# A recurrence and an MLP on one core: two bf16 transposes replaced by one fp32 transpose of channel pairs, with gates made before the turn and a set issue order

## The chip, the cores and the metric

The kernel runs on one core of one Trainium2 chip. The metric is device time in microseconds (us) of the whole program; lower is better. "Span" is the time from the first to the last instruction in a profiled execution, some 2 us less than the timed figure. Before the change the kernel took 444.84 us (median of 2 runs, 444.7 to 444.98).

PE is the matrix engine, PEld its weight loads (they overlap with matmuls), DVE the vector engine, ACT the scalar engine, POOL the general engine, SP the engine that only issues DMA here. SBUF is the on-chip working memory of 128 partitions, PSUM the memory that PE writes.

## The reference

```python
# x, f_logit: (4, 6144, 256) fp32; lower_bound: (256,); w1, w2: (256, 1024); w_out: (1024, 256)
sig = 1.0 / (1.0 + np.exp(-f_logit))
f = lower_bound + (1.0 - lower_bound) * sig
for t in range(S):                       # a recurrence along the tokens, per channel
    h = f[:, t] * h + (1.0 - f[:, t]) * x[:, t]
    y[:, t] = h
out = np.maximum(y @ w1, y @ w2) @ w_out # (24576, 256) fp32
```

Both kernels use u = sigmoid(-f_logit), so that 1 - f = (1 - lower_bound) u, and max(h1, h2) = h1 + relu(h2 - h1). So PE multiplies y by wd (the scaled difference of w2 and w1), ACT takes the relu, and PE multiplies that by w_out and adds y times w13 = w1 w_out.

## The kernel before

Tokens come in 48 blocks of 512. The inputs arrive with tokens on partitions; the recurrence is a scan along the free dimension, so channels have to be on partitions. PE turns both inputs, 128x128 at a time, in bf16 (the load casts from fp32 on the way).

```python
def load(c):                                   # cast to bf16 in the DMA, issued by POOL
    nat = inpool.tile([P, CH // P, D], BF16, name=name)
    nc.gpsimd.dma_start(out=nat[...], in_=src[b, t0:t0 + nt, :].rearrange("(i p) d -> p i d", p=P))
...
def turn(j, slot):                             # two bf16 transposes in each slot
    s, q = divmod(slot, FC // 2)
    if q == 0:
        turned[j, s] = ps_t.tile([P, KC, TB], BF16, name=("fT", "xT")[s])
    for h in range(KC):                        # KC = 2 channel halves
        nc.tensor.transpose(turned[j, s][:, h, q * P:(q + 1) * P],
                            ins[c][s][:, o * NSB + q, h * P:(h + 1) * P], ident_b[:])

def recurrence(j):                             # gates with channels on partitions
    nc.scalar.activation(out=u[:], in_=fT[:], func=AF.Sigmoid, scale=-1.0)
    nc.vector.tensor_tensor(out=v[:], in0=u[:], in1=xT[:], op=ALU.mult)
    for h in range(KC):
        nc.vector.tensor_scalar(out=ff[:, h, :], in0=u[:, h, :], scalar1=nom[:, h:h+1], scalar2=1.0, ...)
        nc.vector.tensor_tensor_scan(out=y[:, h, :], data0=ff[:, h, :], data1=v[:, h, :], ...)
...
# hidden(j, fc): two 128x512 matmuls into dT, relu by ACT into rt
# project(j, slot): five 128x256 matmuls into psO; weights are 128 tokens of y or rt
with tc.manual_schedule(engines={ENG.PE}):     # only PE's order is set, the rest is scheduled
    for j in range(NBLK + 1):
        for fc in range(FC):                   # FC = 8 slots of a block
            if j < NBLK: hidden(j, fc)
            if j > 0: project(j - 1, fc)
            if j + 2 < NBLK: turn(j + 2, fc)
        if j + 2 < NBLK: recurrence(j + 2)
```

## Time and profile before

| before | value | view |
|---|---|---|
| span | 443.3 us | page |
| PE busy | 95% | page, part 1 |
| chain of waits on PE | 94% | page, part 4 |
| a slot with two bf16 transposes | 1.09 us | timeline |
| a slot without any (last two blocks) | 0.975 us | timeline |
| first slot with all its parts (block 1, slot 1) | at 28.08 us | timeline |

The page of the kernel before. Its first line gives busy time, share of the span and number of instructions of each engine; the chain of waits is followed back from the last instruction, as shares of the span by engine and then by line.

```profile
PE 423.0 (95%) x3488; PEld 309.8 (70%) x3488; DVE 247.0 (56%) x345; ACT 278.5 (63%) x442; POOL 44.9 (10%) x57
...
PE 94%; DMA 4%; POOL 1%; DVE 0%; issue 0%; POOLq 0%
PE psO L227 47%; PE dT L202 37%; PE xT L103 5%; PE fT L103 5%; DMA wob<-in_moe_w_out_dram 4%; POOL fn L86 1%; POOL xn L86 1%; PE psO L186 0%; DVE osb L237 0%; POOL ident_f masks.py:199 0%; POOL ident_f masks.py:197 0%; POOLq masks.py:199 0%; POOLq L284 0%
```

PE is the bound. "Busy" alone does not prove it, since the records of matmuls overlap and their ends are modelled. The timeline does. This is PE in a steady stretch of the kernel before (start in us, length in us, engine, line, operation, names, shapes, count):

```profile
300.26 0.27 PE L103 MATMUL fT<-ident_b,fn 128*128 128x128 bf16 x2
300.38 0.59 PE L202 MATMUL dT<-y,wd 128*128 128x512 bf16 x2
300.81 0.71 PE L227 MATMUL psO<-wob,rt 128*128 128x256 bf16 x5
301.35 0.28 PE L103 MATMUL fT<-ident_b,fn 128*128 128x128 bf16 x2
301.46 0.38 PE L202 MATMUL dT<-y,wd 128*128 128x512 bf16 x1
```

Read the starts, not the lengths. A pair of 128x512 matmuls starts at 300.38 and the next at 301.46 (1.09 us when averaged over more slots): that is one slot. No idle time is noted in brackets behind any line. The last blocks have no transposes left to do:

```profile
425.94 0.59 PE L202 MATMUL dT<-y,wd 128*128 128x512 bf16 x2
426.37 0.71 PE L227 MATMUL psO<-wob,rt 128*128 128x256 bf16 x5
426.91 0.59 PE L202 MATMUL dT<-y,wd 128*128 128x512 bf16 x2
```

There a slot takes 426.91 - 425.94 = 0.97 us (0.975 to 0.98 over several slots). The difference of 0.11 us is what two bf16 128x128 transposes cost in the stream: 0.054 us each, although the record of one lasts 0.22 us.

The groups of instructions that the change touches (out<-in, shapes, count, then busy us and mean ns of one, then idle time of the engine before them and what ended it):

```profile
L127 DVE TENSOR_TENSOR_SCAN y<-ff,y,v 128x512 bf16<-128x512 bf16 x88 | 108.2, 1272 | 1.5
...
L103 PE MATMUL fT<-ident_b,fn 128*128 128x128 bf16 x384 | 52.2, 221 | 13.4 <-DVE ident_b L65 13.4
...
L103 PEld LDWEIGHTS <-fn 128*128 128x128 bf16 x384 | 37.3, 99 | 19.2 <-DMA fn<-in_f_logit_dram 11.0
...
L119 DVE TENSOR_SCALAR ff<-u,nom 128x512 bf16<-128x512 bf16 x96 | 29.9, 354 | 25.6 <-ACT u L113 25.6
...
L115 DVE TENSOR_TENSOR v<-u,xT 128x1024 bf16<-128x1024 bf16 x48 | 32.5, 677 | 3.9 <-PE xT L103 3.9
```

### The profile page before, as it was taken

How to read it: one execution, taken by the hardware profiler on the slowest of the kernel's cores; microseconds unless marked ns; L12 is line 12 of the kernel's file. 1: busy time of each engine (PE TensorE's matmuls, PEld its weight loads, DVE VectorE, ACT ScalarE, POOL GpSimd, SP SyncE). 2: the span in 40 equal slices, each digit the busy share in tenths (PEclk: the TensorE clock that was granted, in tenths of full speed). 3: DMA queues.
4: the chain of work that ended last, by engine and by line, in shares of the span. 5: the costliest groups of instructions: out<-in, count | busy, mean ns of one | idle time of the engine just before them, and what ended most of it. 6: DMA issues, size and time to landing. Idle time of an engine off the chain costs nothing.

```text
span 443.3 us, 8434 instructions
## 1 busy us (share of the span) xinstructions
PE 423.0 (95%) x3488; PEld 309.8 (70%) x3488; DVE 247.0 (56%) x345; ACT 278.5 (63%) x442; POOL 44.9 (10%) x57
## 2 busy tenths in 40 slices
PE   0689999999999999999999999999999999999996
PEld 0567777777777777777777777777777777777765
DVE  2744665565556546655655565466546655654631
ACT  3666666666666766666666666666766666666661
POOL 6300101001001001010010010010100100000000
PEclk9999999999999999999999999999999999999999
DMA  8999769487487495694874965956948731212112
GB/s 221 198 198 215 138 124 152 83 146 123 94 140 127 91 163 94 123 151 87 146 119 99 140 121 96 163 95 124 149 85 149 120 95 48 72 49 71 57 64 95
DMA packets 78501, 53.49 MB, mean 121 GB/s; under 512 B 2688, under 2 KB 77440, under 8 KB 78464
## 3 DMA queue, kind: packets, MB, share of 16 engines
q0 software_dynamic: 50992, 25.69, 46.1%
q1 hardware_dynamic: 26384, 25.17, 18.4%
q10 hardware_dynamic: 1088, 2.10, 1.5%
q8 instruction: 27, 0.44, 0.4%
q14 instruction: 10, 0.08, 0.1%
HBM read 53.48 MB, written 25.17 MB: 177 GB/s over the span
## 4 chain that ended last, share of the span: by engine, by line
PE 94%; DMA 4%; POOL 1%; DVE 0%; issue 0%; POOLq 0%
PE psO L227 47%; PE dT L202 37%; PE xT L103 5%; PE fT L103 5%; DMA wob<-in_moe_w_out_dram 4%; POOL fn L86 1%; POOL xn L86 1%; PE psO L186 0%; DVE osb L237 0%; POOL ident_f masks.py:199 0%; POOL ident_f masks.py:197 0%; POOLq masks.py:199 0%; POOLq L284 0%
## 5 line engine op out<-in xcount | busy, mean ns | idle before, releaser
L210 ACT ACTIVATE rt<-dT 128x512 bf16<-128x512 f32 x384 | 226.8, 597 | 142.2 <-PE dT L202 142.1
L227 PE MATMUL psO<-wob,rt 128*128 128x256 bf16 x1536 | 229.8, 273 | 0.0
L202 PE MATMUL dT<-y,wd 128*128 128x512 bf16 x768 | 228.2, 379 | 1.1 <-DVE y L127 1.1
L227 PEld LDWEIGHTS <-rt 128*128 128x128 bf16 x1536 | 150.3, 98 | 57.5
L237 DVE COPY osb<-psO 128x512 f32<-128x512 f32 x96 | 66.4, 692 | 152.5 <-PE psO L227 152.5
L127 DVE TENSOR_TENSOR_SCAN y<-ff,y,v 128x512 bf16<-128x512 bf16 x88 | 108.2, 1272 | 1.5
L227 PE MATMUL psO<-w_182,y 128*128 128x256 bf16 x384 | 73.3, 273 | 0.0
L227 PEld LDWEIGHTS <-y 128*128 128x128 bf16 x384 | 37.6, 98 | 44.4
L103 PE MATMUL fT<-ident_b,fn 128*128 128x128 bf16 x384 | 52.2, 221 | 13.4 <-DVE ident_b L65 13.4
L202 PEld LDWEIGHTS <-wd 128*128 128x128 bf16 x768 | 59.6, 98 | 0.9 <-DVE y L127 0.5
L103 PE MATMUL xT<-ident_b,xn 128*128 128x128 bf16 x384 | 52.2, 221 | 0.0
L113 ACT ACTIVATE u<-fT 128x1024 bf16<-128x1024 bf16 x48 | 49.1, 1024 | 4.9 <-PE fT L103 2.3
L103 PEld LDWEIGHTS <-fn 128*128 128x128 bf16 x384 | 37.3, 99 | 19.2 <-DMA fn<-in_f_logit_dram 11.0
L86 POOL DMA_DIRECT2D fn<-in_f_logit_dram x25 | 21.9, 874 | 237.0 <-PE fT L103 174.2
L119 DVE TENSOR_SCALAR ff<-u,nom 128x512 bf16<-128x512 bf16 x96 | 29.9, 354 | 25.6 <-ACT u L113 25.6
L103 PEld LDWEIGHTS <-xn 128*128 128x128 bf16 x384 | 37.4, 99 | 4.8
L115 DVE TENSOR_TENSOR v<-u,xT 128x1024 bf16<-128x1024 bf16 x48 | 32.5, 677 | 3.9 <-PE xT L103 3.9
L86 POOL DMA_DIRECT2D xn<-in_x_dram x25 | 21.6, 866 | 68.2 <-PE dT L202 64.9
L127 DVE TENSOR_TENSOR_SCAN y<-ff,v 128x512 bf16<-128x512 bf16 x8 | 9.4, 1211 | 0.1
L157 DVE TENSOR_TENSOR wdf<-w2n,w1n 128x1024 f32<-128x1024 f32 x2 | 2.5, 1226 | 6.5 <-DMA w2n<-in_moe_w_dram 6.5
L156 ACT CAST w1b<-w1n 128x1024 bf16<-128x1024 f32 x2 | 2.1, 1045 | 4.6 <-DMA w1n<-in_moe_w_dram 4.6
L186 PE MATMUL psO<-wob,w1T 128*128 128x256 bf16 x16 | 1.9, 272 | 1.8 <-DMA wob<-in_moe_w_out_dram 1.8
(18 smaller groups left out, 15.2 us busy)
## 6 DMA issues: line engine op xcount, KB each, us to landing
out_dram<-osb SPq DMA_DIRECT2D x96, 256.0 KB, 2.7
fn<-in_f_logit_dram POOLq DMA_DIRECT2D x23, 512.0 KB, 8.2
xn<-in_x_dram POOLq DMA_DIRECT2D x23, 512.0 KB, 8.4
w1n<-in_moe_w_dram ACTq DMA_DIRECT2D x2, 512.0 KB, 6.2
w2n<-in_moe_w_dram ACTq DMA_DIRECT2D x2, 512.0 KB, 7.4
fn<-in_f_logit_dram POOLq DMA_DIRECT2D x2, 256.0 KB, 10.3
xn<-in_x_dram POOLq DMA_DIRECT2D x2, 256.0 KB, 10.9
wob<-in_moe_w_out_dram POOLq DMA_DIRECT2D x1, 512.0 KB, 17.0
```

What stands on the lines that cost most here:

```text
L86: nc.gpsimd.dma_start(out=nat[:, 0:ni, :], in_=src[b, t0 : t0 + nt, :].rearrange("(i p) d -> p i d", p=P),)
L103: nc.tensor.transpose(dst[:, h, q * P : (q + 1) * P], ins[c][s][:, o * NSB + q, h * P : (h + 1) * P], ident_b[:],)
L113: nc.scalar.activation(out=u[:], in_=fT[:], func=AF.Sigmoid, scale=-1.0)
L115: nc.vector.tensor_tensor(out=v[:], in0=u[:], in1=xT[:], op=ALU.mult)
L119: nc.vector.tensor_scalar(out=ff[:, h, :], in0=u[:, h, :], scalar1=nom[:, h : h + 1], scalar2=1.0, op0=ALU.mult, op1=ALU.add,)
L127: nc.vector.tensor_tensor_scan(out=y[:, h, :], data0=ff[:, h, :], data1=v[:, h, :], initial=0.0 if prev is None else prev[:, h, TB - 1 : T ...
L156: nc.scalar.copy(out=w1b[:, :, cols], in_=w1n[:, :, cols])
L157: nc.vector.tensor_tensor(out=wdf[:, :, cols], in0=w2n[:, :, cols], in1=w1n[:, :, cols], op=ALU.subtract,)
L202: nc.tensor.matmul(dT[:], lhsT=wd[:, kc, fc * P : (fc + 1) * P], rhs=y[:, kc, :], start=(kc == 0), stop=(kc == KC - 1),)
L210: nc.scalar.activation(out=rt[:], in_=dT[:], func=AF.Relu)
L227: nc.tensor.matmul(ps[:, r, :], lhsT=steps[s][0], rhs=steps[s][1], start=(r == 0 and s == 0), stop=(r == 1 and s == n - 1), skip_group_che ...
L237: nc.vector.tensor_copy(out=osb[:], in_=ps[:])
```

## The change

The intent was to halve the transposes. The inputs are loaded in fp32 without a cast. The gate u and the drive v = u x are made while tokens are still on partitions, and written as bf16. Two neighbouring channels then form one 4-byte word, and PE turns a block of 128 tokens by 128 words as if it were fp32: one transpose moves what two did. The vector engine reads the halves of the words out of PSUM with a step of two. Channels 2p and 2p+1 now share partition p, so the weights are loaded in that order too. The projection takes every second token as weights, so that two output rows of one partition are next to each other in memory. All engines' orders are set by hand, and the weights' preparation at the start was rewritten.

```diff
-        nat = inpool.tile([P, CH // P, D], BF16, name=name)         # gpsimd, cast
+        fn = inpool.tile([P, NQ, D], FP32, name="fn")               # no cast
...
+    def gate(j):
+        u = natpool.tile([P, NQ * D], BF16, name="un")
+        nc.scalar.activation(out=u[:], in_=fn[:]..., func=AF.Sigmoid, scale=-1.0)
+    def drive(j):
+        nc.vector.tensor_tensor(out=v[:], in0=u[:], in1=xn[:]..., op=ALU.mult)
...
-        for h in range(KC):
-            nc.tensor.transpose(dst[:, h, q * P : (q + 1) * P],
-                ins[c][s][:, o * NSB + q, h * P : (h + 1) * P], ident_b[:])
+        turned[j, s] = ps_t.tile([P, TB], FP32, name=("uT", "vT")[s])
+        nc.tensor.transpose(turned[j, s][:, q * P : (q + 1) * P],
+            src[:].bitcast(FP32)[:, q * P : (q + 1) * P], ident[:])
...
+    def half(j, s, h):
+        return turned[j, s][:].bitcast(BF16).rearrange("p (t h) -> p h t", h=KC)[:, h, :]
+    # forget() and scan() read half(j, 0, h) and half(j, 1, h) straight from PSUM
...
-        tok = slice(i * P, (i + 1) * P)
+        tok = slice(2 * g * P + r, 2 * (g + 1) * P, 2)
...
-    with tc.manual_schedule(engines={ENG.PE}):
+    with tc.manual_schedule():                                      # every engine
+        (loads; gate(0), drive(0), turns, forget and scan of block 0)
+        for g in range(2):
+            for h in range(KC):
+                scale_w1(g, h)                                      # ACT
+                diff(g, h)                                          # DVE
+            for h in range(KC):
+                turn_w1(g, h)                                       # PE, copy by ACT
+        gate(1)
+        drive(1)
+        (turns of block 1)
+        for h in range(KC):
+            forget(1, h)
+            scan(1, h)
+        (wob casts on POOL; gate(2), drive(2); then the blocks, w13 made inside block 1)
```

## The prediction

> **What bounds the kernel now.** PE. The page has it busy 95% of the 443.3 us span, the chain of waits is 94% PE, and the clock is at 1.0. The timeline shows no gap: in steady state one block of 512 tokens takes 8.71 us, eight slots of 1.09 us, each two 128x512 matmuls, five 128x256 and two bf16 128x128 transposes. The last two blocks have no transposes and their slots take 0.98 us, so one bf16 transpose costs 0.054 us of PE. ACT (63%) and DVE (56%) follow. The first full block starts at 26.9 us; before it the PE waits for data (the w_out load takes 17 us to land).
>
> **Removed.** Two channels travel as one 4-byte word, so a slot has one fp32 128x128 transpose in place of two bf16 ones. If an fp32 transpose takes one pass like a bf16 one, a slot costs 0.98 + 0.054 = 1.035 us and a block 8.28: 0.435 us less, 19.6 us over 45 blocks. The trace before has no fp32 transpose. The Trainium skill, "TensorE: Matmul & The Clock Gate", Terms, says that transpose_mode made fp32 4x faster, which I take for one pass instead of four; no run here shows it yet. The same page (Weight-path perf modes) keeps the fast weight load from fp32, but the new load sits behind a 128x512 matmul of 0.215 us and should hide. Weights of the projection now step by two tokens; that page allows such steps with the fast load, and there are 0.109 us per matmul to hide in.
>
> **Added, off the critical path.** The drive multiplies an fp32 operand: 1.23 us like the 128x1024 f32 subtraction, instead of 0.68. The forget factors read PSUM with a stride: about 0.65 instead of 0.31-0.35. DVE per block, an estimate from these durations: scans 2.5, copies 1.4, forget 1.3, drive 1.2 = 6.4 of 8.28 us. ACT stays at 5.6. DMA reads the same HBM bytes, without a cast.
>
> **The start.** Everything on one hardware queue, in fixed order. ACT takes the gates of blocks 2 and 3 ahead of block 0's evictions, so these wait for loads 11 and 13 of 512 KB. The page's rate in the first slices (cast loads at their HBM size) is about 320 GB/s, so load 13 lands near 24 us; block 1 starts near 27 us, and its 1.75 us of w13 matmuls now come inside it: some 1.5 us later than before.
>
> **Sum.** 28.5 + 45 x 8.28 + 2 x 7.84 + 4.4 + 4 (end) = 425 us span, 427 us as timed (-4%). Range 419 to 445. Faster by over 2%: 0.75; within 2%: 0.17; slower: 0.08.
>
> **What would show it right.** Timeline: slots of 1.03-1.04 us, one transpose each; blocks of 8.28 us; PE still over 93% of the chain; DVE near 78%, ACT near 66%; no new PE wait on DVE or ACT in steady state; first full block at 26-29 us.
>
> **What would make it wrong.** (1) The fp32 transpose costs more than one pass or its weight load shows: at 0.11 us a slot is 1.09 and nothing is gained (444 us); at four passes (0.22) it is 1.20 and the time some 485. (2) Strided weight loads exceed 0.109 us: all 1920 projection matmuls stretch. (3) DVE's PSUM reads are slower than thought, and PE waits for the scans. (4) The start is longer, by up to 5 us, because one queue moves less than 320 GB/s.

## The result, and the profile after

The changed kernel took 450.58 us (median of 2 runs, 450.28 to 450.88), against 444.84. Ratios here are the mean time of one kernel's fast runs over that of the other's of the same rounds, so not quite the ratio of the medians: 1.0127, with a 95% interval of 1.0098 to 1.0157. The change costs 1.3% (under 2%, but clear of the noise), and the prediction of 427 us (419 to 445) was wrong. Executions over 1.5% slower than the fastest of the same kernel are left out of the means.

The page after, the lines that answer to those of before:

```profile
PE 429.6 (96%) x3104; PEld 323.6 (72%) x3104; DVE 302.1 (67%) x344; ACT 277.9 (62%) x441; POOL 69.2 (15%) x96
...
PE 94%; DMA 2%; ACT 1%; DVE 1%; SPq 0%; issue 0%
PE psO L206 47%; PE dT L177 37%; PE vT L128 5%; PE uT L128 5%; DMA w1n<-in_moe_w_dram 2%; PE dT L265 1%; ACT w1s L247 1%; PE psO L277 0%; DVE vn L120 0%; DVE y L162 0%; SPq L226 0%; ACT w1T L268 0%; ACT un L100 0%; SPq L82 0%; DVE osb L217 0%
```

PE is as busy and as much of the chain as before. The stretch of the timeline that answers to the one of before:

```profile
299.85 0.59 PE L177 MATMUL dT<-y,wd 128*128 128x512 bf16 x2
300.28 0.27 PE L128 MATMUL vT<-ident,vn 128*128 128x128 f32 x1
300.39 0.71 PE L206 MATMUL psO<-wob,rt 128*128 128x256 bf16 x5
300.93 0.59 PE L177 MATMUL dT<-y,wd 128*128 128x512 bf16 x2
301.36 0.27 PE L128 MATMUL vT<-ident,vn 128*128 128x128 f32 x1
```

There is one transpose in a slot now, as intended. But the pairs of 128x512 matmuls start at 299.85 and 300.93: the slot is still 1.09 us. From the transpose's start at 300.28 to that of the next matmul are 0.11 us, where a bf16 one took half of that. Worked out in ns from the records of both traces (60 to 420 us), the mean from start to start is 109.2 for the fp32 transpose, the same as for a bf16 128x256 matmul, and 55.8 for each bf16 transpose. The groups that answer to those of before:

```profile
L162 DVE TENSOR_TENSOR_SCAN y<-ff,y,vT 128x512 bf16<-128x512 bf16 x88 | 108.0, 1267 | 52.5 <-PE vT L128 52.4
L149 DVE TENSOR_SCALAR ff<-uT,nom 128x512 bf16<-128x512 bf16 x96 | 67.8, 746 | 60.6 <-PE uT L128 60.6
...
L128 PE MATMUL uT<-ident,un 128*128 128x128 f32 x192 | 53.0, 283 | 8.9 <-ACT un L100 7.6
L120 DVE TENSOR_TENSOR vn<-un,xn 128x1024 bf16<-128x1024 bf16 x48 | 58.5, 1219 | 4.4 <-DMA xn<-in_x_dram 2.8
...
L128 PEld LDWEIGHTS uT<-ident,un 128*128 128x128 f32 x192 | 27.9, 147 | 32.2 <-issue 6.8
```

On DVE the drive went from 677 to 1219 ns and the forget factor from 354 to 746 ns, while the scan kept its time. PE did not wait for any of it in the steady state. What is left is the start:

```profile
22.39 1.06 PE L177 MATMUL dT<-y,wd 128*128 128x512 bf16 x2
24.70 0.45 PE L128 MATMUL uT<-ident,un 128*128 128x128 f32 x1 [1.25 <-DVE ff L149]
24.94 1.06 PE L177 MATMUL dT<-y,wd 128*128 128x512 bf16 x2
25.80 0.42 PE L128 MATMUL uT<-ident,un 128*128 128x128 f32 x1
26.01 1.06 PE L177 MATMUL dT<-y,wd 128*128 128x512 bf16 x2
...
30.76 0.59 PE L177 MATMUL dT<-y,wd 128*128 128x512 bf16 x2
...
31.30 0.59 PE L177 MATMUL dT<-y,wd 128*128 128x512 bf16 x2
...
31.84 1.91 PE L277 MATMUL psO<-wob,w1T 128*128 128x256 bf16 x16
...
34.27 0.27 PE L206 MATMUL psO<-w,y 128*128 128x256 bf16 x1 [0.41 <-DVE w L284]
...
34.70 0.59 PE L177 MATMUL dT<-y,wd 128*128 128x512 bf16 x2
```

In the kernel before the corresponding lines are:

```profile
23.51 1.91 PE L186 MATMUL psO<-wob,w1T 128*128 128x256 bf16 x16 [1.83 <-DMA wob<-in_moe_w_out_dram]
...
27.00 0.59 PE L202 MATMUL dT<-y,wd 128*128 128x512 bf16 x2
...
28.08 0.59 PE L202 MATMUL dT<-y,wd 128*128 128x512 bf16 x2
```

Block 1 starts (its first pair of 128x512 matmuls) at 31.30 us instead of 27.00 (the prediction's 26.9), and its second slot, the first that has all its parts without the work of the start in between, at 34.70 instead of 28.08: 6.6 us later. From there to the copy of the last output are 445.02 - 34.70 = 410.3 us after and 439.30 - 28.08 = 411.2 before. So the balance is: 6.6 us lost at the start, 0.9 won in the other 410 us, 5.7 us slower, as timed.

Three things are to be read from the lines of the start. First, PE stands still before 24.70: the bracket says it waited 1.25 us for the forget factor. Second, PE runs at half pace in block 0: the pair of 24.94 is followed by the transpose at 25.80, so one 128x512 matmul takes 0.43 us and a slot 1.07; at 34.70 the same pair is followed after 0.43 us, 0.215 each. Third, w13 is now made inside block 1 (31.84), and a projection waits 0.41 us for its copy (34.27); before, that work was done ahead of block 1 (23.51). PE of the kernel before was at full pace when its block 0 began: from 13.38 us on it turned blocks 0 and 1 and the weights almost without a pause, and eight bf16 transposes took 1.01 us at 13.38 but 0.61 at 16.62.

### The profile page after: what moved, and what is told of

It reads as the page before. It is cut to its first block, busy times and chain, and to the rows that moved or that the text cites. A ratio compares the mean times of both kernels' runs of the same rounds, so it can differ in the third digit from the quotient of the medians.

```text
span 449.0 us, 8126 instructions
## 1 busy us (share of the span) xinstructions
PE 429.6 (96%) x3104; PEld 323.6 (72%) x3104; DVE 302.1 (67%) x344; ACT 277.9 (62%) x441; POOL 69.2 (15%) x96
## 3 DMA queue, kind: packets, MB, share of 16 engines
q1 hardware_dynamic: 19424, 32.51, 21.5%
## 4 chain that ended last, share of the span: by engine, by line
PE 94%; DMA 2%; ACT 1%; DVE 1%; SPq 0%; issue 0%
PE psO L206 47%; PE dT L177 37%; PE vT L128 5%; PE uT L128 5%; DMA w1n<-in_moe_w_dram 2%; PE dT L265 1%; ACT w1s L247 1%; PE psO L277 0%; DVE vn L120 0%; DVE y L162 0%; SPq L226 0%; ACT w1T L268 0%; ACT un L100 0%; SPq L82 0%; DVE osb L217 0%
## 5 line engine op out<-in xcount | busy, mean ns | idle before, releaser
L162 DVE TENSOR_TENSOR_SCAN y<-ff,y,vT 128x512 bf16<-128x512 bf16 x88 | 108.0, 1267 | 52.5 <-PE vT L128 52.4
L149 DVE TENSOR_SCALAR ff<-uT,nom 128x512 bf16<-128x512 bf16 x96 | 67.8, 746 | 60.6 <-PE uT L128 60.6
L177 PEld LDWEIGHTS <-wd 128*128 128x128 bf16 x768 | 75.9, 99 | 10.0 <-issue 1.0
L206 PE MATMUL psO<-w,y 128*128 128x256 bf16 x384 | 73.4, 273 | 0.4 <-DVE w L284 0.4
L128 PE MATMUL uT<-ident,un 128*128 128x128 f32 x192 | 53.0, 283 | 8.9 <-ACT un L100 7.6
L120 DVE TENSOR_TENSOR vn<-un,xn 128x1024 bf16<-128x1024 bf16 x48 | 58.5, 1219 | 4.4 <-DMA xn<-in_x_dram 2.8
L128 PE MATMUL vT<-ident,vn 128*128 128x128 f32 x192 | 52.6, 281 | 0.7 <-DVE vn L120 0.7
L100 ACT ACTIVATE un<-fn 128x1024 bf16<-128x1024 f32 x48 | 50.4, 1050 | 2.8 <-DMA fn<-in_f_logit_dram 2.8
L128 PEld LDWEIGHTS uT<-ident,un 128*128 128x128 f32 x192 | 27.9, 147 | 32.2 <-issue 6.8
L128 PEld LDWEIGHTS vT<-ident,vn 128*128 128x128 f32 x192 | 27.7, 146 | 23.6 <-DVE vn L120 1.5
```

The costliest lines, as they stand in the source:

```text
L100: nc.scalar.activation(out=u[:], in_=fn[:].rearrange("p q d -> p (q d)"), func=AF.Sigmoid, scale=-1.0)
L120: nc.vector.tensor_tensor(out=o, in0=u, in1=xi, op=ALU.mult)
L128: nc.tensor.transpose(turned[j, s][:, q * P : (q + 1) * P], src[:].bitcast(FP32)[:, q * P : (q + 1) * P], ident[:],)
L149: nc.vector.tensor_scalar(out=ffs[j][:, h, :], in0=half(j, 0, h), scalar1=nom[:, h : h + 1], scalar2=1.0, op0=ALU.mult, op1=ALU.add,)
L162: nc.vector.tensor_tensor_scan(out=ys[j][:, h, :], data0=ffs[j][:, h, :], data1=half(j, 1, h), initial=0.0 if prev is None else prev[:, h, ...
L177: nc.tensor.matmul(dT[:], lhsT=wd[:, kc, fc * P : (fc + 1) * P], rhs=y[:, kc, :], start=(kc == 0), stop=(kc == KC - 1),)
```

## The experiments

Fifteen kernels ran. All gave correct results. Each is shown with the main lines of its change against the changed kernel, abridged, or described where the lines would repeat. The changed kernel itself was timed only in the first two runs, so differences to it are across rounds and chips; the kernel before, timed beside every one of them, had medians of 444.84 to 445.09 us. Two sets of theories were open: why a slot did not get shorter, and why the start got longer.

### Why the slot is as long as before

**e2_bf16: only the fp32 transposes undone.**

```diff
-        nc.tensor.transpose(turned[j, s][:, q*P:(q+1)*P], src[:].bitcast(FP32)[:, q*P:(q+1)*P], ident[:])
+        for h in range(KC):
+            nc.tensor.transpose(turned[j, s][:, h, q*P:(q+1)*P],
+                src[:].rearrange("p (q w h) -> p h q w", h=KC, q=NQ)[:, h, q, :], ident_b[:])
... (the PSUM tile and half() follow suit)
```

> The changed kernel with only the fp32 transposes undone: each becomes two bf16 128x128 transposes of the same words, everything else (fp32 loads, gates with tokens on partitions, strided projection weights, order) as changed. Theory A (an fp32 128x128 transpose streams at half the rate of a bf16 one, 0.109 us against 0.054, so the exchange is even): slots stay 1.09 us, time 449 to 452 us. Rival R (the fp32 transpose costs 0.054 and the other 0.054 us per slot comes from the token-strided weight loads or another part of the change): slots 1.14 us and some 470 us.

Measured: 449.76 us (4 runs, 449.16 to 450.42), ratio to before 1.0105. PE in a steady slot of this kernel:

```profile
200.00 0.59 PE L179 MATMUL dT<-y,wd 128*128 128x512 bf16 x2
200.44 0.28 PE L130 MATMUL uT<-ident_b,un 128*128 128x128 bf16 x2
...
201.09 0.59 PE L179 MATMUL dT<-y,wd 128*128 128x512 bf16 x2
```

The slot stays at 1.09 us. So the exchange of two bf16 transposes for one fp32 transpose is even, and nothing else in the change (strided token weights, order, fp32 loads) costs PE time in the steady state. Theory A holds and rival R falls.

**e4_double: each fp32 transpose twice.**

```diff
+        for _ in range(2):
             nc.tensor.transpose(turned[j, s][...], src[:].bitcast(FP32)[...], ident[:])
```

> The changed kernel with every fp32 transpose issued twice (same input, same output). Theory A: the second costs as much as the first, 0.109 us of PE: slots 1.20 us, blocks 9.58 us, +39 us over 45 blocks, some 490 us. Rival S (0.054 us of streaming and a penalty of 0.054 for each switch between bf16 and fp32): no switch between the two, so +0.054 per slot: slots 1.14 us, some 470 us. Rival W (bound by the fp32 weight load, whose record lasts 0.142 us): +0.14 per slot, slots 1.23 us, some 502 us.

Measured: 489.85 us (1 run, and so of unknown state). PE in a steady slot of this kernel:

```profile
200.72 0.59 PE L178 MATMUL dT<-y,wd 128*128 128x512 bf16 x2
201.16 0.38 PE L129 MATMUL vT<-ident,vn 128*128 128x128 f32 x2
201.37 0.38 PE L207 MATMUL psO<-w,y 128*128 128x256 bf16 x2
...
201.92 0.59 PE L178 MATMUL dT<-y,wd 128*128 128x512 bf16 x2
```

The slot is 201.92 - 200.72 = 1.20 us, 0.11 more than with one. Two transposes take 201.37 - 201.16 = 0.21 us. The second needs no switch from bf16 to fp32 and costs as much as the first, so rival S falls. Against W speak the 0.11 us in place of 0.14, and the changed kernel's own timeline, which shows when the load of a single transpose ends:

```profile
200.09 0.14 PEld L128 LDWEIGHTS uT<-ident,un 128*128 128x128 f32 x1
200.30 0.27 PE L128 MATMUL uT<-ident,un 128*128 128x128 f32 x1
```

The load begins at 200.09, under the second 128x512 matmul, and ends at 200.23; the transpose begins at 200.30. It did not wait for its weights, and still it takes 0.11 us until the next matmul. Nor is it the load of the next weights: in e4 an fp32 load (0.14 us) follows the first transpose and a bf16 load (0.10) the second, and both transposes take 0.109. What is left is the streaming of the identity itself: 0.109 us for 128 fp32 columns, twice the bf16 time. It also doubles when PE runs at half pace, as the matmuls do (25.80 to 26.01 in the start shown above: 0.21 us). That it is the stream was reached by excluding the others. A transpose with fewer moving columns would show it directly; this last step was argued and not shown.

**e3_fp32mm: the same without transpose mode.**

```diff
-        nc.tensor.transpose(turned[j, s][...], src[:].bitcast(FP32)[...], ident[:])
+        nc.tensor.matmul(turned[j, s][...], lhsT=src[:].bitcast(FP32)[...], rhs=ident[:], start=True, stop=True)
```

> The changed kernel with the fp32 transposes as ordinary fp32 matmuls against the identity, without transpose mode (the packed pairs may come out inexact, so the result may be wrong on purpose). It measures what transpose mode saves. If it is 4 times faster, as the skill says, and a transpose takes 0.109 us: 0.436 us each, slots 1.42 us, some 568 us. If the ordinary one is 4 bf16 streams (0.22 us): slots 1.20 us, some 490 us, and transpose mode saves a factor of 2 only.

Measured: 490.65 us (1 run, of unknown state), and the result was correct. The groups of the turn of u:

```profile
L128 PE MATMUL uT<-ident,un 128*128 128x128 f32 x384 | 74.9, 281 | 10.9 <-ACT un L100 7.6 <-DVE ff L151 1.7
```

384 matmuls stand where 192 instructions were issued: an ordinary fp32 matmul is split in two, each with its own weight load, and each costs what one fp32 transpose costs. The slot grows to 1.20 us, so it takes 1.20 - 0.98 = 0.22 us, four times a bf16 transpose. Transpose mode takes half of that, two times a bf16 one. This is where the prediction went wrong.

### Why the start is longer

Theory H: the half pace of PE in block 0. Theory O: the set order, which makes block 1's gate late and holds the PSUM bank of u. Theory L: block 0 waits for its loads, whatever PE and the order do. Each of the next five runs was timed in 3 rounds beside the kernel before (444.98 to 445.09 us there).

**e5_warm2: unneeded matmuls while PE is idle.**

```diff
             for h in range(KC):
                 turn_w1(g, h)
+            dummy(8)     # 8 bf16 128x256 matmuls of the identity into an unused PSUM tile
```

> About the start, where the changed kernel loses 6.7 us (first matmuls of block 2 at 42.3 us against 35.6) and gets 1.0 back afterwards. The changed kernel with eight unneeded 128x256 bf16 matmuls after each half of the weight turns, in time in which PE is idle. Theory H (PE runs at half clock through block 0, 22.4 to 30.1 us: 512-column matmuls at 0.427 us, because it was little used before): it runs at full rate when block 0 comes, its slots go from 1.07 to about 0.65 us (ACT's 0.6 then bounds), about 2.5 to 3 us less, some 447.5 us. Rival L (block 0 is bound by the loads of blocks 2 and 3 and the gates ahead of the evictions): under 0.5 us.

Measured: 449.0 us, but spread from 446.84 to 450.6 over four runs, where the changed kernel's two lie 0.6 us apart. PE was at full pace by 17 us, then stood still for about 2 us before block 0's first transpose, and in the profiled run (the slowest) it was back at half pace from 24 to 29.9 us; the granted clock of that window is 0.62:

```profile
22.00:31.00 9.00, 7.13 (x24) 3.76 (x25) 6.71 (x7) 5.10 (x9) 3.81 (x6) 0.62 1.05 352
```

The line gives the length of the window, busy us and count of PE, PEld, DVE, ACT and POOL, then the granted clock, the DMA share and GB/s. In the changed kernel the granted clock of block 0 reads 1.00 at the same half pace, so for a start the spacing of matmuls is the safer reading. The run decides little: at best 3.7 us were won, which is against L, at worst nothing.

**e14_forget_first: the PSUM bank of u freed sooner.**

```diff
         for h in range(KC):
             forget(1, h)
+        for h in range(KC):
             scan(1, h)
```

> The changed kernel with one thing moved at the start: both forget factors of block 1 before its two scans, nothing else. It frees the PSUM bank of u 1.3 us sooner, so the stall of 1.8 us before block 0's first transpose shrinks to about 0.5. If only the stall matters: 1 to 1.5 us less than the changed kernel, some 449 us. If the gap is also what lets PE fall back to, or stay at, half clock through block 0: 3 to 5 us less, 446 to 447 us, and 512-column matmuls at 0.215 us from before 25 us on. The gates and weight turns keep their old order, so it should not reach the 445.3 us of the run with the whole new order of the start.

Measured: 448.05 us (447.38 to 448.76), 2.5 us less than the changed kernel: more than the stall alone. It lies between the two forecasts. The gap before 24.7 us is gone, and full pace comes at 25.6 us instead of 30.1.

**e17_forget_warm: both of these.**

> The changed kernel with the forget factors of block 1 ahead of its scans (448.05 us alone) and eight unneeded matmuls after each half of the weight turns (449.0 alone). If the half clock is a cost of its own once the gap is closed: 512-column matmuls at 0.215 us through block 0 and 1.3 to 2 us less than 448.05: 446 to 447 us, with little spread. If not: 448 us.

Measured: 446.99 us (446.21 to 447.9), with an interval of 1.0026 to 1.0065 against e14's 1.0053 to 1.0082. With the gap closed, the matmuls of block 0 run at full pace from the first one, and the median is 1.1 us lower. So half pace costs something of its own (H), though the intervals overlap a little. Single profiles of the start need care here: the second half of w1 landed at 11.44 us in e14's profiled run and at 10.38 in e17's, without any change to the loads, and all that follows moves with it. Counted from that landing, block 1's second slot comes after 20.40 and 19.44 us, so 0.96 us are the edit's. The gap before block 0's first transpose (1.91 us in e5_warm2, 0.32 here) is also what the edit took from e5_warm2, whose profiled run fell back to half pace.

**e6_order2: another order at the start.**

```diff
         for g in range(2):
             for h in range(KC):
                 scale_w1(g, h)
                 diff(g, h)
-            for h in range(KC):
-                turn_w1(g, h)
         gate(1)
         drive(1)
+        turn_w1(0, 0); turn_w1(0, 1); turn_w1(1, 0)
         (turns of block 1)
+        turn_w1(1, 1)
         for h in range(KC):
             forget(1, h)
+        for h in range(KC):
             scan(1, h)
```

> The changed kernel with another order at the start only: all four weight scalings first, then the gate and drive of block 1 before the last weight turns, and both forget factors of block 1 before its scans, so the PSUM bank of u comes free before the first scan instead of after it. Theory O (the set order costs the start: the stall of 1.8 us before 24.7 us and the late gate of block 1 at 19.0): block 0 starts about 3 us earlier and the time falls by 2 to 4 us. Theory L: no change, as block 0 waits for loads.

Measured: 445.31 us (445.23 to 445.5), ratio to before 1.0006 (0.9991 to 1.0021): 5.3 us less than the changed kernel, with a few moved lines and no extra work. It does better than expected: in its profiled run block 0 begins 3.0 us sooner (19.37 us instead of 22.39), as forecast, and PE is at full pace by 21.4 us. Theory L falls: the loads are the same and in the same order.

**e9_order_warm2: that order with unneeded matmuls.**

```diff
         turn_w1(1, 0)
+        dummy(8)
         (turns of block 1)
```

> Both changes of the start together (eight unneeded matmuls before block 1 is turned). If H and O hold and are separate costs: 5 to 6 us less than the changed kernel, about 445 us, the time of the kernel before, as the steady slots are equal. If they share a cause: no more than the better of the two.

Measured: 446.74 us, 1.4 us more than without them. This was a miss: the order had already warmed PE, and the eight matmuls now stood in front of the turns of block 1. They waited 1.4 us for a PSUM buffer that ACT had not yet emptied, and the turns begin at 18.78 us instead of 15.53. So the two gains do not add: this order had removed the half pace already. It does not do so every time: e12 and e15 below begin in the same order, and in their profiled runs block 0 ran at half pace until about 26.2 and 26.7 us.

The start explains all of the loss. In each profiled run, the span minus the start of block 1's second slot is the steady part, and it depends on the kind of transpose alone:

| kernel | span, us | block 1, slot 1 at | difference |
|---|---|---|---|
| before (bf16 pairs) | 443.3 | 28.08 | 415.2 |
| e2_bf16 (bf16 pairs) | 448.6 | 33.36 | 415.2 |
| changed (fp32) | 449.0 | 34.70 | 414.3 |
| e5_warm2 | 448.5 | 34.17 | 414.3 |
| e14_forget_first | 446.2 | 31.84 | 414.3 |
| e17_forget_warm | 444.1 | 29.82 | 414.3 |
| e9_order_warm2 | 445.2 | 30.85 | 414.3 |
| e6_order2 | 443.4 | 29.10 | 414.3 |

(The differences are taken before rounding.) The fp32 transposes win 0.9 us over the run, some 2.4 ns in each of 360 slots (2 x 55.8 - 109.2), and the start loses 6.6.

### Whether PE time taken from a slot does come back

The prediction took for granted that a slot that is shorter on PE makes the kernel shorter. To test this, the turn of v was taken from PE and given to a DMA transpose (SBUF to SBUF), whose layout code the changed kernel already has, unused.

**e7_dma_v: from block 2 on, the old start.**

```diff
-    by_dma_v = lambda j: False
+    by_dma_v = lambda j: j >= 2
...
                         drive(j + 3)
+                        turn_dma(j + 3, 1)       # abridged; and no turn_pe(j + 2, 1, q)
```

> The changed kernel with the drive v turned by a DMA transpose from the second block on, u still by PE in fp32. If PE is the bound and the DMA keeps up: four of eight slots lose 0.109 us, blocks 8.28 us, 19.6 us less: some 431 us. If the DMA transposes are slow or hold up the stores in their queue, PE waits for y and the gain is gone.

Measured: 434.7 us in one run, of unknown state. That is 15.9 us less than the changed kernel, of 19.6 expected, but see the next two.

**e10_dma_order_warm2: with the start of e9.**

> The DMA transposes of v (434.7 us in one run) with the start of the run before: the gains are in different stretches and should add, 429 to 431 us. With DMA at over 90% busy in that run, an earlier start could instead lead to longer waits for the turned v later: then 432 to 435.

Measured: 438.78, 463.54, 457.17 and 440.34 us. Only the first and the last count as fast; both lie above either forecast. Their ratio to before is 0.9876, but no kernel without DMA transposes spreads like this.

**e13_dma_all: with the start of e6, no unneeded matmuls.**

> As before with v turned by DMA in all blocks from block 2 on, no warm-up matmuls. By PE alone 20.0 us less than 445.3: 425 us. The run with the unneeded matmuls took 439 to 464 us, so if DMA is the bound this one is spread as widely and no better than the one with two of three blocks; if the unneeded matmuls were the cause, it is steady at 425 to 430.

Measured: 473.13, 439.07, 504.19 and 455.04 us; only the second counts as fast, and it is about the time of e12 below. So the unneeded matmuls were not the cause. The profile of e10, a fast run, shows another limit. Its DMA row (mean busy share of the 16 DMA engines in 40 slices, in tenths) and the group of the scans that read v turned by DMA:

```profile
DMA  8997799999999999999987978988998999833312
...
L162 DVE TENSOR_TENSOR_SCAN y<-ff,y,vTs 128x512 bf16<-128x512 bf16 x86 | 105.6, 1270 | 46.9 <-DMA vTs<-vn 46.9
```

The DMA engines have next to no slack (9 is 90% or more), and DVE stood still 46.9 us for turned v. That the slow runs come from this too was not tested; what can be said is that no kernel with DMA slack showed such a spread.

**e11_dma_half and e12_dma_2of3: in every second block, and in two of three, from block 2 on, with the start of e6.**

> The better order of the start (445.3 us), no warm-up, and v turned by DMA in the even blocks from block 2 on (23 of 46). PE loses 4 x 0.109 us in each of these: 10.0 us, 435 us, with the spread of fast runs under 1 us, because DMA falls from over 90% busy to about 75%.

> As the run before with v turned by DMA in two of three blocks: 30 or 31 blocks, 13.3 us less than 445.3: 432 us if DMA at some 83% still keeps up; slower than that and spread over several us if it does not.

Measured: 443.92 us (443.02 to 444.51) and 439.93 us (439.49 to 440.55). Both are steadier, so DMA keeps up, but both miss, by 9 and 8 us. The trace of e11 shows where: the first transpose is issued at 23.14 us, behind the loads of the coming blocks, and lands 15.8 us later, so PE stands idle near 40 us (3.3 us at the longest) and loses its full pace again. In e12's profiled run the half pace in block 0 adds to it. From 57 us on, two blocks take 16.95 us together, as expected.

**e15_half_late and e16_2of3_late: the same, from block 8 on.**

```diff
-    by_dma_v = lambda j: j >= 2 and j % 3 != 0
+    by_dma_v = lambda j: j >= 8 and j % 3 != 0
```

> The better order of the start, and v turned by DMA in the even blocks from block 8 on (20 blocks). If PE time taken from a slot comes back one for one: 20 x 0.435 = 8.7 us less than 445.3, 436.6 us. If waits take it back: nearer 440.

> As the run before with two of three blocks from block 8 on (27 blocks): 11.7 us less than 445.3, 433.6 us, if DMA keeps up; more and spread if it does not.

Measured: 438.43 us (437.14 to 438.91) and 434.09 us (433.88 to 435.79). Against 445.31 us these win 6.9 and 11.2 us, where 8.7 and 11.7 were expected; e16 is at 0.9764 of the kernel before (0.9742 to 0.9787), and e15 at 0.9848. What e15 lacks lies at the start: in its profiled run, the slowest of four, block 0 ran at half pace until about 26.7 us and block 1's second slot came at 31.25 us, 2.1 later than in e6, with the same code up to there. From that slot to the end e15 takes 405.8 us and e16 402.9, where e6 takes 414.3: 8.5 and 11.4 us less. So PE time taken from a slot comes back nearly one for one as long as DMA has slack. Three blocks of e16, in three stretches:

```profile
90.00:115.35 25.35, 25.35 (x187) 18.80 (x185) 18.50 (x22) 16.98 (x28) 4.49 (x6) 1.00 0.76 210
200.00:225.35 25.35, 25.35 (x187) 18.85 (x186) 18.33 (x21) 16.98 (x28) 4.49 (x6) 1.00 0.89 209
300.00:325.35 25.35, 25.35 (x187) 18.74 (x185) 18.38 (x23) 16.93 (x28) 4.49 (x6) 1.00 0.73 211
```

PE is busy all through each window, DVE for 18.3 to 18.5 of 25.35 us, and the DMA share moves between 0.73 and 0.89: PE is the bound again. Version e16_2of3_late beats both kernels.

## Why the prediction was wrong

**The bound: right.** PE bounds both kernels; it has 94% of the chain in both.

**The step that failed.** It is the sentence "If an fp32 transpose takes one pass like a bf16 one, a slot costs 0.98 + 0.054 = 1.035 us and a block 8.28". The mechanism (half as many transposes) was right and came about. The term that was mis-sized is the cost of one fp32 transpose: 0.109 us instead of 0.054. The saving per block was 0.02 us instead of 0.435, and 0.9 us over the run instead of 19.6. The basis was the entry of the Trainium skill, "TensorE: Matmul & The Clock Gate", Terms, that transpose_mode is 4x faster for fp32. I read it as four passes becoming one at bf16 speed. On this chip an ordinary fp32 matmul against the identity costs 0.22 us and a transpose in that mode half of it, so the factor is two against an ordinary fp32 matmul, and the cost is still twice that of bf16. The number in the page was a ratio, and no trace here showed its base. The prediction's own list had this case as its first risk, with the right slot (1.09 us) and 444 us, but gave it too little weight: the range ended at 445. Of the 23.6 us between the 427 predicted and the 450.6 measured, this step makes up 18.7 (19.6 - 0.9), and the start, which follows, the other 5.

**The start: wrong in size and cause.** The prediction had it 1.5 us later; the first full slot came 6.6 us later. The loads, which it feared, were as fast as it had reckoned: the page shows 368 and 345 GB/s in the second and third slice, and load 13 landed at 23.6 us (24 predicted). What it left out was the pace of PE. The Trainium skill, same page, Part 1, says that PE falls to half its clock when little used and needs about 3.4 us of busy time to get full pace; this trace agrees on the half (0.43 against 0.215 us per 128x512 matmul), but not on the 3.4 us (see the last section). A start in which PE has little to do therefore makes the first dense block slow as well. It also left out that DVE runs forget, scan, forget, scan in the set order, which keeps a PSUM bank occupied that PE's next transpose needs, and that w13 costs 2.3 us inside block 1, with the wait for its copy, and not 1.75.

**The weights that step by two tokens: right.** Their loads are recorded at 98 ns before and after, and e2 shows that they cost nothing. This is as the Trainium skill has it (same page, Weight-path perf modes).

**DVE and the others: right that it does not matter, nearly right in size.** The drive took 1.22 us (1.23 predicted), the forget factor 0.746 (0.65 predicted, without a source). DVE was busy for 67% of the span and ACT for 62% (78 and 66 predicted, for a shorter span). PE waited for no engine in the steady state.

**The end of 4 us and the blocks without transposes: right**; the last two blocks still have slots of 0.975 us.

## What to carry to other kernels

In a stream bound by PE, count what an instruction takes from start to start between its neighbours. Fewer instructions of a wider type are no gain when each takes twice as long, so measure that rate in one small run before rebuilding a data flow around it. After a change of order, compare the time of the first full slot as well as the steady slot: here the steady part was even and the start decided. Work that PE does not have to do can go to an engine with slack, but only up to where that slack ends, and not while the first loads are still queued. And a start whose pace differs from run to run can hide or feign a gain of 2 us, so compare such variants from the first steady slot on.

## What the Trainium skill lacked or had wrong

- "TensorE: Matmul & The Clock Gate", Terms: "4× faster for FP32" of transpose_mode. Here an fp32 128x128 transpose costs 0.109 us in a warm stream, an ordinary fp32 matmul of the same shape 0.22 us (2x) and a bf16 transpose 0.056 us. The page gives no cost of an fp32 transpose against a bf16 one.
- The same page does not say that an ordinary fp32 matmul is recorded as two matmuls with two weight loads (384 for 192 issued, e3_fp32mm).
- The same page, Part 1, puts the change to full clock near 4 us of sustained matmuls, with 0.5 us of variation. In the changed kernel PE worked almost without a gap from 24.7 us and reached full pace only at 30.1 us, 5.4 us later. Counted in the same way, from block 0's first transpose, it took some 3.7 us in e2_bf16 and 6 in e5_warm2.
- "Advanced Engine Details and Errata", X-Bar Transpose (TRN2), says that transpose DMAs are as fast as regular ones, with 350 to 400 GB/s. An estimate from e16's page: its hardware queue took 35.4% of 16 engines for 432.4 us, the changed kernel's 21.5% for 449.0, so 27 transposes of 256 KB took 905 us of one engine, or 2.1 us of all sixteen each: about 125 GB/s. The same queue without transposes moved 32.51 MB at some 337 GB/s while busy. Other traffic ran beside both.
